# Linear attention with its gradients: eight stores issued by GpSimd instead of ScalarE, and a minimum moved from VectorE to GpSimd

## The chip, the cores and the metric

The kernel runs on one core of a Trainium2 chip. The metric is device time in microseconds (us) of one execution; a kernel's time is the median of its runs. In the profile PE is TensorE (PEld its weight loads), DVE is VectorE, ACT is ScalarE, POOL is GpSimd, and SP is SyncE, which computes nothing and issues transfers. ACTq, POOLq and SPq are the sequencers of these engines, which issue transfers.

## What is computed

The program takes two attention blocks over the same sequence length, S = 2048 rows of D = 448 columns, 16 heads of 28, and gives the output and all gradients in bfloat16.

```python
def _A_ref(x, wqkv, wo):                       # block A: linear attention
    qkv = split_heads(x @ wqkv)                # q, k, v
    phi = lambda t: jnp.where(t > 0, t + 1, jnp.exp(t)) + 1e-6
    pq, pk = phi(q), phi(k)
    kv = jnp.einsum("bhsd,bhse->bhde", pk, v)
    z = jnp.einsum("bhsd->bhd", pk)
    num = jnp.einsum("bhqd,bhde->bhqe", pq, kv)
    den = jnp.einsum("bhqd,bhd->bhq", pq, z)[..., None] + 1e-6
    return merge_heads(num / den) @ wo
def _B_ref(x, wq, wk, wv, wo):                 # block B: softmax attention, one k and v for all heads
    ...
out = concatenate([_A_ref(...), _B_ref(...)], axis=-1); grads = vjp(grad_out)
```

The listing is shortened from the reference (`split_heads` and `merge_heads` stand for its reshapes). Outputs: out_0 the forward result, out_1 the gradient of A's x, out_2 that of A_wqkv (448 x 1344: columns for q, k, v), out_3 that of A_wo, out_4 to out_8 those of block B. The change lies in block A: in the derivative of phi for q, and in the stores of the v columns of out_2 and of out_3.

## The kernel before

Block A is worked first (`phase_A`), then the projections of block B (`phase_B_pre`), then a long loop over block B's attention, forward and backward at once, in 512 steps, then B's remaining gradients. By the profile, A with the projections of B takes the first 210 us and the attention loop nearly all the rest. The sequence is cut into NS = 16 tiles of 128 rows. Each engine runs its own instructions strictly in order. Their order on each engine is set by a scheduler from the order of the program and the dependences, so instructions of neighbouring steps are interleaved; waits between engines go by semaphores. Work tiles come from small rotating pools: `psA` holds four PSUM buffers of each name ("agen" for products used at once, "aacc" for accumulators), `awk` three SBUF buffers of each name ("osb", "phiT"). A new tile waits until the readers of the tile that last had its buffer are done; where that reader is a store, until the store has landed.

The parts that the change and the prediction touch, in order of time:

- **Projections** (L270 to L287). For each tile `kproj` and, five tiles later, `qproj` multiply x by the weights (L236) into an "agen" buffer. `phi` takes the exponential on ACT (L241), its minimum with 1 plus 1e-6 on DVE (L243), and max(value, 0) plus that on DVE (L244), which also frees the PSUM buffer. For q the exponential stays in `wq_n` (the trace calls it wdq), and L262 replaces it there by its minimum with 1: that is the derivative of phi. `wq_n` is next read at L349 (`den_rx`), tile by tile.
- **kv and the denominators** (L282 to L364). `hilo` (L249 on ACT, L250 on DVE) takes the sums of phi(k) and x apart into two bfloat16 parts, `blkprod` multiplies them with the weights and masks the result on DVE (L301).
- **The loop over tiles** L399 to L411: forward result, the gradient of q, accumulated products.
- **Query gradient of the weights** (`gw(gqn, 0)`, L452), the gradient of k (L455 to L461, with L460 on DVE), loads for block B: B_x transposed by four transfers of SP (L467, issued at L115; the tile is called pk), B_wo by 16 loads (L474), four transposes of the gradient of k (L480, issued at L98; tile gaT).
- **Value and output weight gradients** (L481 to L497), four tiles i: `by_heads` (L484, matmuls at L313) gives the v columns of out_2; ACT evicts them into "osb" (L486) and issues the store (L487); matmuls with G (L493) give out_3; ACT evicts into "phiT" (L496) and issues the store (L497).
- **GpSimd's preparations for block B** (L499 to L515): memsets of `rep` (L501) and `wq_pad` (L502), 16 small copies (L505, L506), four copies (L509), memsets of `bsel` (L512, L515).
- **Key gradient of the weights** (`gw(gkn, 1)`, L524), evicted by ACT (L446, "osb" again, and L442) and stored by GpSimd (L447); then GpSimd loads B's output gradient into xa (L525, issued at L94). SP transposes rep and wq_pad (L522, L527).
- **Gradient of x** (L529 to L539): 11 matmuls a tile, evicted by ACT (L536), stored by GpSimd (L538).

Of the kernel before, what the change touches and what calls it, by code (L numbers as in the profile page):

```python
# [9 lines left out]
ALU = mybir.AluOpType  # L10
# [6 lines left out]
D = 448  # L17
P = 128
# [7 lines left out]
def kernel(  # L26
# [21 lines left out]
    nc = tc.nc  # L48
# [31 lines left out]
    def mm(out_ap, lhsT, rhs, start=True, stop=True):  # L80
        nc.tensor.matmul(out_ap, lhsT=lhsT, rhs=rhs, start=start, stop=stop, tile_position=(0, 0))  # L81
# [15 lines left out]
    def dma_T(dst, src, t0, n):  # L97
        nc.sync.dma_start_transpose(dst[:, t0:t0 + n, :, :].rearrange("p t c k -> p (t c) k"),  # L98
                                    src[:, t0:t0 + n, :].rearrange("p t d -> p (t d)"))
# [17 lines left out]
    def chunks_of(i):  # L117
        lo, hi = HR[i]
        return [k for k in range(4) if k * P < hi and k * P + DC_ROWS[k] > lo]
# [4 lines left out]
    def phase_A(pa, cA, cB, awk, psA):  # L124
        def gen(shape, dt=F32):
            return psA.tile(shape, dt, name="agen")
# [4 lines left out]
        def big(nm):  # L131
            return cA.tile([P, NS, 512], BF16, name=nm)

        xa, ga, pq, pk, wq_n, ppB = (big(n) for n in ("xa", "ga", "pq", "pk", "wdq", "pqpT"))
# [98 lines left out]
        def proj(st, off):  # L233
            ps = gen([P, D])
            for c in range(4):
                mm(ps[:, :], xaT[:, st, c, :], w3[:, c, off:off + D], start=(c == 0), stop=(c == 3))  # L236
            return ps

        def phi(ps, dst, E):

            nc.scalar.activation(out=E, in_=ps[:, :], func=ACT.Exp)  # L241
            tm = awk.tile([P, D], BF16, name="phiT")
            nc.vector.tensor_scalar(out=tm[:], in0=E, scalar1=1.0, scalar2=1e-6, op0=ALU.min, op1=ALU.add)  # L243
            nc.vector.scalar_tensor_tensor(out=dst, in0=ps[:, :], scalar=0.0, in1=tm[:], op0=ALU.max, op1=ALU.add)  # L244
# [14 lines left out]

        def qproj(st):  # L260
            phi(proj(st, 0), pq[:, st, 0:D], wq_n[:, st, 0:D])
            nc.vector.tensor_scalar(out=wq_n[:, st, 0:D], in0=wq_n[:, st, 0:D], scalar1=1.0, scalar2=None, op0=ALU.min)  # L262
            if st % 4 == 3:
                dma_T(tT, pq, st - 3, 4)

# [4 lines left out]
        for st in range(NS):  # L270
            if st + 2 < NS:
                xT(st + 2)
            kproj(st)
            if st >= 4:
                nc.scalar.activation(out=zero[st - 4], in_=zrow[:, :], func=ACT.Copy)
            if st >= 2:
                accmm(k1acc, xa, pk, st - 2)
            if st >= LAG:
                qproj(st - LAG)
# [6 lines left out]
        for st in range(NS - LAG, NS):  # L286
            qproj(st)  # L287
# [15 lines left out]
        def cols(t, k, i):  # L303
            if id(t) in blk_at:
                return blks[:, (blk_at[id(t)] + k) * D + i * P:(blk_at[id(t)] + k) * D + (i + 1) * P]
            return t[:, k, i * P:(i + 1) * P]

        def by_heads(ps, pairs):
            n = 4 * len(pairs)
            for m in range(n):  # L310
                lhs, rhs = pairs[m // 4]
                lo, hi = HR[m % 4]
                nc.tensor.matmul(ps[:, lo:hi], lhsT=lhs(m % 4), rhs=rhs[:, m % 4, lo:hi], start=(m == 0), stop=(m == n - 1),  # L313
                                 tile_position=(0, 0), skip_group_check=True)
# [166 lines left out]
        for i in range(4):  # L481
            r = DC_ROWS[i]
            ps = gen([P, D])
            by_heads(ps, [(lambda k: K1[0][:, i, k, :], dkv_blk), (lambda k: K1[1][:, i, k, :], dkv_blk)])  # L484
            sb = awk.tile([P, 512], BF16, name="osb")[:, 0:D]
            nc.scalar.activation(out=sb[0:r, :], in_=ps[0:r, :], func=ACT.Copy)  # L486
            nc.scalar.dma_start(out_2[i * P:i * P + r, 2 * D:3 * D], sb[0:r, :])  # L487
            ps = gen([P, 512])
            ks = chunks_of(i)
            n = 0  # L490
            for j in range(2):
                for k in ks:
                    mm(ps[:, :], cols(kv_blk, k, i), G[j][:, :, k, :], start=(n == 0), stop=(n == 2 * len(ks) - 1))  # L493
                    n += 1
            sb = awk.tile([P, D], BF16, name="phiT")
            nc.scalar.activation(out=sb[0:r, :], in_=ps[0:r, 0:D], func=ACT.Copy)  # L496
            nc.scalar.dma_start(out_3[i * P:i * P + r, :], sb[0:r, :])  # L497

        wq_pad = K1[0].rearrange("p c h k -> p c (h k)")  # L499
        rep = K1[1].rearrange("p c h k -> p (c h k)")[:, 0:1024].rearrange("p (w c k) -> p w c k", w=2, k=P)  # L500
# [6 lines left out]
        for c in range(4):  # L507
            r = slice(64 if c == 3 else 0, P)
# [131 lines left out]
    with ExitStack() as pa:  # L640
        cA = pa.enter_context(tc.tile_pool(name="cA", bufs=1, side="right"))
        cB = pa.enter_context(tc.tile_pool(name="cB", bufs=1, side="right"))
        awk = pa.enter_context(tc.tile_pool(name="awk", bufs=3, side="right"))
        io = phase_A(pa, cA, cB, awk, psA)
        pn3, shifts = phase_B_pre(pa, cA, awk, psA, io)
# [5 lines left out]
    with ExitStack() as cs_:  # L651
# [265 lines left out]
        with tc.manual_schedule():  # L917
            nc.sync.dma_start(wo, wo_d[:, 0:D].rearrange("(g p) c -> p g c", p=P))
            qX[0] = pqa_.tile([P, 4, 2, 512], BF16, name="qX")
            for g in range(4):  # L920
                st = pd_.tile([P, 2, 512], BF16, name="dsT").rearrange("p a (n j) -> p a n j", j=32).rearrange(
                    "p a (n b) j -> p (a n) b j", b=4)
# [3 lines left out]
            for u in range(NU + 28):  # L926
# [48 lines left out]
                if (b := due(u, 27)) is not None:  # L975
                    qc, pair, g, hp = blk(b)
                    nc.vector.tensor_scalar(out=qT_B[g][64 * hp:64 * hp + 64, qc * 256:(qc + 1) * 256],  # L977
                                            in0=oq[64:128, 0:256], scalar1=scale, scalar2=None, op0=ALU.mult)
# [20 lines left out]
                if u % 2:  # L999
                    b, i = divmod(u - 27, 8)  # L1000
# [25 lines left out]
                if u == 536:  # L1026
                    dk_sum = pd_.tile([P, 2, 512], BF16, name="dsT").rearrange("p a b -> p (a b)").bitcast(F32)
                    for c in range(2):
                        r = 64 * (1 - c)
# [5 lines left out]
                if 0 <= y < NU:  # L1035
                    b, tp = divmod(y, 8)
                    if tp == 0:
                        dsx[b] = px_.tile([P, 8, 2, 2, 256], BF16, name="dsx")
                    nc.vector.transpose(  # L1039
                        out=dsx[b][:, tp, :, :, :].rearrange("p h t c -> p (h t c)").bitcast(F32),  # L1040
# [15 lines left out]
        for c in range(4):  # L1056
# [4 lines left out]
                                           op0=ALU.mult, op1=ALU.add)  # L1061
# [47 lines left out]
        for c in range(4):  # L1109
            r = DC_ROWS[c]  # L1110
# [41 lines left out]
```

## Time and profile before

| | |
|---|---|
| runs (3) | 1057.06 us median, 1056.17 to 1061.49 |
| profiled execution | 1055.19 us, of which its span on the core 1053.5 |
| granted TensorE clock | 0.999 |
| busy in the span, PE, DVE, ACT, POOL | 1008.2, 898.1, 871.2, 772.8 us |
| 16 x L262 on DVE | 264 to 377 ns each, median 266; from 17.4 to 49.6 us |
| 40 to 60 us: PE, DVE busy of 20 us | 18.27, 18.98 |
| 120 to 140 us: PE, ACT, POOL busy of 20 us | 17.14, 5.06, 9.07 |
| DMA busy share, 100 to 180 us in steps of 20 | 1.03, 0.91, 1.09, 1.06 |

All lines of the profile are of one execution; times run from the start of its span. An instruction group shows engine, line and operation, out<-in and the shape. In brackets stands the idle time of the engine just before it, and what released it. The chain of work that ended last is followed back from the last instruction, at each step to what released it. The spans of GpSimd are rougher than those of the other engines.

### The profile page before, as it was taken

The page shows a single profiled execution, that of the slowest core. Times are in us where ns is not written, and L with a number is a line of the kernel's source. Part 1 is how long each engine was busy: PE and PEld are TensorE (multiplying, and loading weights), DVE is VectorE, ACT ScalarE, POOL GpSimd, SP SyncE. Part 2 cuts the span into 40 slices and gives each one's busy share as a digit, 9 for nine tenths or more (in the row PEclk, how much of TensorE's full clock was granted, in tenths as well). Part 3 has the DMA queues.
Part 4 walks back from the last instruction along what each step waited for, and adds up shares of the span by engine and source line. Part 5 has one row for each costly group of instructions (what it writes and reads, how often), then busy time and mean ns, then how long its engine had stood idle before and what let it go on. Part 6 is the DMA issues. An engine that isn't in the chain of part 4 may idle for free.

```text
span 1053.5 us, 40033 instructions
## 1 busy us (share of the span) xinstructions
PE 1008.2 (96%) x16245; PEld 485.7 (46%) x16245; DVE 898.1 (85%) x1797; ACT 871.2 (83%) x1743; POOL 772.8 (73%) x1020
## 2 busy tenths in 40 slices
PE   9999989998999999999999999999999999999997
PEld 5555545434444444444444444444444444444444
DVE  7897500669999999999999999999999999999942
ACT  6463122599999999999999999999999999999632
POOL 6001252238988998899899889988998999888860
PEclk9999999999999999999999999999999999999999
DMA  9879999089999999999999999999999999999972
GB/s 264 157 128 196 188 202 233 21 166 197 200 186 197 177 193 199 199 196 192 193 180 194 196 201 187 199 201 184 188 194 186 196 191 198 201 194 180 216 157 84
DMA packets 689730, 195.15 MB, mean 185 GB/s; under 512 B 670408, under 2 KB 687584, under 8 KB 689544
## 3 DMA queue, kind: packets, MB, share of 16 engines
q1 hardware_dynamic: 680392, 179.97, 101.7%
q0 software_dynamic: 4192, 8.66, 3.0%
q10 hardware_dynamic: 4960, 3.96, 1.2%
q8 instruction: 127, 2.08, 0.8%
q14 instruction: 59, 0.48, 0.2%
HBM read 12.60 MB, written 10.84 MB: 22 GB/s over the span
## 4 chain that ended last, share of the span: by engine, by line
PE 43%; ACT 33%; issue 14%; DVE 5%; POOL 3%; DMA 1%; ACTq 0%; DVEq 0%; SPq 0%; POOLq 0%
ACT cp L960 17%; ACT eT L992 13%; PE agen L81 13%; PE aacc L676 10%; PE agen L676 10%; PE aacc L81 6%; POOL dsT L961 2%; ACT eT L946 2%; PE aacc L809 2%; PE aacc L840 1%; DVE dsT L958 1%; DVE dsx L1039 1%; DMA pk<-in_B_x_dram 0%; DMA out_dram<-dsT 0%; PE aacc L85 0%
## 5 line engine op out<-in xcount | busy, mean ns | idle before, releaser
L961 POOL TENSOR_TENSOR dsT<-cp,eT 128x512 bf16<-128x512 bf16 x512 | 587.8, 1156 | 77.4 <-ACT cp L960 71.2
L1039 DVE STREAM_TRANSPOSE dsx<-dsT 128x512 f32<-128x512 f32 x512 | 357.6, 699 | 2.4 <-POOL dsT L961 0.2
L676 PEld LDWEIGHTS <-R 32*128 32x128 bf16 (+1 forms) x9104 | 228.3, 94 | 274.0 <-issue 238.9
L958 DVE TENSOR_TENSOR dsT<-agen,eT 128x512 bf16<-128x512 f32 x512 | 341.7, 667 | 10.3 <-PE agen L676 5.1
L960 ACT ACTIVATE cp<-agen 128x512 bf16<-128x512 f32 x512 | 314.9, 615 | 11.4 <-PE agen L676 10.3
L946 ACT ACTIVATE eT<-aacc 128x512 bf16<-128x512 f32 x512 | 313.2, 612 | 13.1 <-PE agen L676 4.1
L992 ACT ACTIVATE eT<-aacc 128x512 bf16<-128x512 f32 x512 | 321.0, 627 | 0.0
L676 PE MATMUL agen<-dsx,qX 32*32 32x512 bf16 x4024 | 264.1, 376 | 0.0
L676 PE MATMUL agen<-doT,R 32*128 32x256 bf16 x2048 | 246.5, 269 | 3.9 <-DVE dsT L958 2.4
L676 PE MATMUL aacc<-R,R 32*128 32x256 bf16 (+1 forms) x2240 | 218.2, 268 | 6.8 <-DVE oTs L819 1.9
L676 PE MATMUL agen<-eT,R 128*32 128x256 bf16 x2048 | 157.5, 274 | 0.1
L676 PE MATMUL agen<-dsT,R 128*32 128x256 bf16 x2048 | 156.6, 274 | 0.1
L676 PEld LDWEIGHTS <-qX 32*32 32x32 bf16 x4096 | 78.3, 89 | 111.7 <-issue 53.5
L676 PE MATMUL aacc<-eN,don 128*32 128x512 bf16 x1024 | 97.0, 379 | 0.0
L81 PEld LDWEIGHTS <-R 128*128 128x128 bf16 x517 | 40.9, 98 | 41.9 <-issue 11.8
L427 POOL COPY pk<-R 128x256 bf16<-128x256 bf16 x4 | 1.6, 398 | 71.4 <-DVE R L389 61.9
L81 PE MATMUL agen<-R,R 128*128 128x448 bf16 (+1 forms) x180 | 42.1, 361 | 0.5 <-DVE pq L244 0.3
L851 POOL COPY qst<-R 128x512 bf16<-128x512 bf16 x56 | 34.3, 613 | 3.6 <-DMA qX<-qst 3.5
L823 POOL TENSOR_TENSOR prod<-R,oTs 128x128 f32<-128x128 bf16 x64 | 27.5, 430 | 9.3 <-DVE oTs L819 9.3
L676 PEld LDWEIGHTS <-don 128*32 128x32 bf16 x1024 | 33.8, 97 | 0.7 <-issue 0.3
L586 DVE TENSOR_TENSOR osb<-R 32x512 bf16<-32x512 bf16 x4 | 1.7, 414 | 35.4 <-ACT R L583 35.4
L977 DVE TENSOR_SCALAR R<-agen 64x256 bf16<-64x256 f32 x64 | 27.3, 426 | 2.8 <-PE agen L676 0.8
(232 smaller groups left out, 954.4 us busy)
## 6 DMA issues: line engine op xcount, KB each, us to landing
out_dram<-osb ACTq DMA_DIRECT2D x19, 112.0 KB
eN<-eT SPq DMA_TRANSPOSE x128
xa<-in_A_x_dram SPq DMA_DIRECT2D x8, 224.0 KB
ga<-in_grad_out_dram SPq DMA_DIRECT2D x4, 448.0 KB
xa<-in_grad_out_dram POOLq DMA_DIRECT2D x4, 448.0 KB, 8.5
out_dram<-wdq POOLq DMA_DIRECT2D x8, 224.0 KB, 5.9
eT<-in_grad_out_dram SPq DMA_DIRECT2D x4, 448.0 KB
eT<-in_B_x_dram SPq DMA_DIRECT2D x4, 448.0 KB
```

The source lines that it names most:

```text
L81: nc.tensor.matmul(out_ap, lhsT=lhsT, rhs=rhs, start=start, stop=stop, tile_position=(0, 0))
L676: nc.tensor.matmul(out, lhsT=lhsT, rhs=rhs, start=start, stop=stop, tile_position=pos, skip_group_check=True)
L809: nc.tensor.transpose(onp[:, qb, :, :].rearrange("p h c -> p (h c)"), oTs[0:64, qb * P:(qb + 1) * P], identF[0:64, 0:64], tile_position=(0 ...
L823: nc.gpsimd.tensor_tensor(out=prod[b][:], in0=dnv, in1=os_, op=ALU.mult)
L851: eng.tensor_copy(out=st.rearrange("p (b s) a j -> p b s a j", s=2)[:, :, s, :, :], in_=src.unsqueeze(2).to_broadcast([P, 4, 4, 32]))
L946: nc.scalar.activation(out=eT(u)[:, 0, :], in_=sp[0][:, :], func=ACT.Exp, scale=scale)
L958: nc.vector.tensor_tensor(out=dst[:, 0, :], in0=dp[0][:, :], in1=ew[:, 0, :], op=ALU.mult)
L960: nc.scalar.activation(out=cp[:, :], in_=dp[1][:, :], func=ACT.Copy)
L961: nc.gpsimd.tensor_tensor(out=dst[:, 1, :], in0=cp[:, :], in1=ew[:, 1, :], op=ALU.mult)
L977: nc.vector.tensor_scalar(out=qT_B[g][64 * hp:64 * hp + 64, qc * 256:(qc + 1) * 256], in0=oq[64:128, 0:256], scalar1=scale, scalar2=None, ...
L992: nc.scalar.activation(out=eT(u)[:, 1, :], in_=sp[1][:, :], func=ACT.Exp, scale=scale)
L1039: nc.vector.transpose(out=dsx[b][:, tp, :, :, :].rearrange("p h t c -> p (h t c)").bitcast(F32), in_=dsT[y][:, :, :].rearrange("p h c -> p ...
```

## The change

In `qproj`, L262 runs on GpSimd instead of VectorE: it takes the minimum of the exponentials with 1 in place, for all 16 tiles. In the loop over the value and output weight gradients, the stores L487 and L497 are issued by GpSimd instead of ScalarE, eight in all. What is computed stays the same.

```diff
         def qproj(st):
             phi(proj(st, 0), pq[:, st, 0:D], wq_n[:, st, 0:D])
-            nc.vector.tensor_scalar(out=wq_n[:, st, 0:D], in0=wq_n[:, st, 0:D], scalar1=1.0, scalar2=None, op0=ALU.min)
+            nc.gpsimd.tensor_scalar(out=wq_n[:, st, 0:D], in0=wq_n[:, st, 0:D], scalar1=1.0, scalar2=None, op0=ALU.min)
...
             nc.scalar.activation(out=sb[0:r, :], in_=ps[0:r, :], func=ACT.Copy)
-            nc.scalar.dma_start(out_2[i * P:i * P + r, 2 * D:3 * D], sb[0:r, :])
+            nc.gpsimd.dma_start(out_2[i * P:i * P + r, 2 * D:3 * D], sb[0:r, :])
...
             nc.scalar.activation(out=sb[0:r, :], in_=ps[0:r, 0:D], func=ACT.Copy)
-            nc.scalar.dma_start(out_3[i * P:i * P + r, :], sb[0:r, :])
+            nc.gpsimd.dma_start(out_3[i * P:i * P + r, :], sb[0:r, :])
```

On each engine the order of the remaining instructions is the same as before, but for one pair on PE (weights and matmul of the masked product kvT, 128x168) that comes after the last q projection instead of before it. On GpSimd the 16 minima stand after the memset L564, ahead of the copies L427. The eight stores stand thus: the first two ahead of L501, three among the copies L505 and L506, and three between L502 and the last L506.

## The prediction

> **What bounds the kernel now.** I read the page first, then the waits by stage, then the timelines where a wait of PE stood.
>
> ```profile
> PE 1008.2 (96%) x16245; PEld 485.7 (46%) x16245; DVE 898.1 (85%) x1797; ACT 871.2 (83%) x1743; POOL 772.8 (73%) x1020
> PE 43%; ACT 33%; issue 14%; DVE 5%; POOL 3%; DMA 1%; ACTq 0%; DVEq 0%; SPq 0%; POOLq 0%
> ```
>
> The first line is busy time of each engine, the second the chain of work that ended last. PE is nearly always busy; DVE and DMA hold 5% and 1% of the chain. The change touches only the linear-attention stage, the first 210 us of 1053.5. There PE runs almost without a hole up to 210 us, and whatever follows takes its start from PE (the exponentials of the attention loop start at 210.35 us, after a matmul). So the change is worth the PE holes that it closes, less those that it opens. The two holes that matter stand in the waits of 128 to 138 us and in the chain of 40 to 52 us.
>
> ```profile
> ACT phiT L496 <- DMA pk<-in_B_x_dram: 4.5, 1, 4.5
> PE agen L81 <- ACT phiT L496: 2.9, 1, 2.9
> ```
>
> ```profile
> 129.43 0.54 ACT L486 ACTIVATE osb<-agen 128x448 bf16<-128x448 f32 x1 [2.55 <-PE agen L313]
> 134.04 0.34 ACTq L487 DMA_DIRECT2D out_dram<-osb  x1
> 134.48 0.55 ACT L496 ACTIVATE phiT<-agen 128x448 bf16<-128x448 f32 x1 [4.50 <-DMA pk<-in_B_x_dram]
> ```
>
> The first fence is the waits (total, times, longest); the second ACT's timeline. ACT evicts the first value-gradient tile at 129.43, and its next instruction is the issue of that tile's store. The issue goes out only at 134.04. In the program's instruction list it waits on a completion semaphore which the fourth transpose of B_x (L115, issued by SP at 129.34) also raises. Behind it stands the eviction L496, which frees one of the four "agen" PSUM buffers, and PE needs that buffer: PE stops after the third by_heads (131.59 + 0.63 = 132.2) and goes on at 135.07. That is 2.86 us by the timeline.
>
> ```profile
> 46.13 0.62 DVE pq L244
> 46.75 0.18 DVE wdq L262
> 46.93 0.37 DVE phiT L243 x2
> 47.30 0.53 DVE pq L244
> 47.84 0.18 DVE wdq L262
> 48.02 0.53 DVE pq L244
> 48.55 0.18 DVE wdq L262
> 48.73 0.18 DVE phiT L243
> 48.92 0.21 DVE blks L301
> 49.13 0.53 DVE pq L244
> 49.66 0.18 DVE wdq L262
> 49.84 0.25 DVE blks L301
> 50.14 1.53 PE aacc L81 x24
> ```
>
> This is the chain itself (start, length). From 43.6 to 50.1 us it lies on DVE: the last five q projections are finished there, and the first products of kv wait for L301 behind them. L262, the minimum that moves, is on the chain with 0.18 us a time (its duration is 0.27, but the next instruction starts 0.18 after it). PE's holes there are 0.32, 1.09 and 0.31 us.
>
> **The minimum, part by part.** Removed from DVE: 16 instructions of 0.27 us. Eleven lie in the loop of 17 to 42 us, where PE sets the pace (2.27 to 2.5 us an iteration) and DVE idles up to 0.53 us before L243: they gain nothing. Of the other five, the chain has 0.06 + 4 x 0.18 = 0.78 us.
>
> Added to GpSimd: 16 minima of 128x448 bf16. The trace has no such instruction there. The nearest rows are L509, a GpSimd copy of the same shape with one input, 0.562 us, and L190, a select, 0.553; the far end is L961, 128x512 with two inputs, 1.156. I take 0.56, the row of the same shape and number of inputs. GpSimd ends its setup at 18.6 us and does nothing until 72.2, so no instruction is queued behind the minima but the copies L427 (four, from 72.2). Their reader, L349, starts at 54.5 us; the last minimum, whose L243 is at 48.65, ends some 0.7 us after it. So the new wait of L349 is met before it comes up.
>
> The hidden price is that DVE's L243 may have to wait for GpSimd. The trace shows that such instructions do:
>
> ```profile
> 115.55 0.47 DVE L460 TENSOR_SCALAR phiT<-pk 128x448 bf16<-128x448 bf16 x1
> 116.46 0.26 DVE L460 TENSOR_SCALAR phiT<-pk 128x448 bf16<-128x448 bf16 x1
> 117.18 0.53 DVE L460 TENSOR_SCALAR phiT<-pk 128x448 bf16<-128x448 bf16 x1
> ```
>
> ```profile
> 115.42 0.47 POOL L454 MEMSET ga<- 64x448 bf16 x1
> 117.12 0.47 POOL L454 MEMSET ga<- 64x448 bf16 x1 [1.24 <-issue]
> ```
>
> L460 has L243's shape and kind. Alone it takes 0.26; begun under a GpSimd memset it ends 0.12 to 0.13 us after the memset does. L244 and L461, which read PSUM, show no stretch (0.60 to 0.62). So I lay the minima between the L243s. In the loop, a minimum starts when L243 of q ends and runs beside L244 (0.54 to the next start): it ends as the next L243 begins, costing nothing. In the tail, two L243 stand together, then two L244 (1.08 us), against two minima (1.12 us) that start after the second L243: L243 of tile 13 and of 15 may each slip by 0 to 0.1 us. With m for one minimum, the first L301 can't start before about 45.4 + 4m + 0.6 us: 48.2 for m = 0.56, against 48.1 from DVE alone and 48.84 now. I take a gain of **0.7 us**; the ends are 0.8 and, for m = 1.156, 50.6 - 48.8 = a loss of 1.8.
>
> [...]
>
> **The stores, part by part.** Removed from ACT: eight issues, 0.34 to 1.14 us each, and their waits. With L487 and L497 gone, L496 of tile 0 follows its matmul at about 130.0 and the PSUM buffer is free at 130.6, before PE asks at 132.2. What is late next? L486 and L496 of tiles 1 to 3 take 0.54 us each, against 1.2 us of PE work; nothing. The second stall of ACT (5.38 us before L496 at 145.06) hides under PE's 9.24 us of the key gradient and costs nothing already. The gain is the whole hole, **2.86 us**.
>
> Added to GpSimd: eight issues, by the L447 rows 0.55 us each, 4.4 us. In the instruction list the first two stand ahead of the memset L501, the next three among the copies L505/L506, the last three after the memset L502. Laid end to end from 130.0: L501 at 131.2, the last copies at 138.2, L502 to 140.0, the store of tile 3's value gradient at 141.1, L509 to 144.1, L515 to 146.8, the key gradient's stores to 149.0, the loads of xa (L94) 149.0 to 152.1. Now those loads issue at 150.65 to 153.7. Nothing is pushed back; rep (read by PE at 181.8) and wq_pad (read by SP's transposes at 161.4) keep 15 us or more. SP's queue keeps its order.
>
> New waits: the evictions L446 of the key gradient reuse "osb" buffers, and now wait for stores that GpSimd issued late. The third needs tile 3's store, issued at 141.1; stores of 112 KB from GpSimd landed in 3.7 us (median of L447's six), 4.8 in the stretch of 141 to 153 us, so at 146 against the 145.0 at which PE has the sum. One us is covered: behind these evictions stand L442 and the L536s, and PE has four PSUM buffers of 2.08 us each before it needs them. The cover ends at about 154 us, a landing 11 us after issue; the largest median landing of the trace's GpSimd groups is 8.5 (448 KB). So its cost runs from nothing to nothing within the rows.
>
> Do 3.6 us survive to the end? Transposes keep DMA full to 183 us and won't come sooner, but their readers have room: gkT's second transpose landed at 144.4, needed at 155; the transposes of B's output gradient are issued by 184, read at 211. The load of wo (209.8) follows PE. In the attention loop every transfer follows the loop's own engines, so its start carries through.
>
> **Sum.** 0.7 + 2.86 = 3.6 us. The profiled execution took 1055.19 us (span 1053.5 and 1.7 around it): 1051.6. It lay 1.9 under the median of the runs, 1057.06; against the median the forecast is 1057.06 - 3.6 = **1053.5**.
>
> **Rivals.** [...] (b) *The shift is lost*: a transfer that PE doesn't wait for now ends as late as before and PE waits for it before the loop: 1057. For it: DMA full from 100 to 183 us; against: the 10 to 25 us of room. A store that doesn't start sooner is no rival, since PE waits only for ACT. [...]
>
> **Chances.** Forecast 0.69, (a) 0.13, (b) 0.09, (c) 0.09. More than 4.6 us can't come from PE's holes (1.7 at 46 to 50, 2.9 at 132). A run of this kernel can tell about 0.5% (5.3 us) from no change; 3.6 is under that, but the runs scatter (1056.17 to 1061.49), and I give 0.23 to a measured gain past it, all of it out of the forecast's 0.69. So faster 0.23, within 0.5% 0.68, slower 0.09. Range: down to 1050.5 (4.6 us and 2 of scatter), up to 1057.3 for (a) and (b).
>
> **What would show it.** L496 of tile 0 near 129 us on ACT with no DMA before it, and no PE hole of 2.9; L85's second group about 3.6 us before 146.86; the first exponentials at 206.8 instead of 210.35. For the minimum: L262 on POOL at 0.56, L243's maximum after 20 us still under 0.4, PE's 1.09 us hole at 48 to 49 down to 0.3. Wrong if L262 takes over 1 us, if L446's third eviction waits past 150 us, or if the start of the loop moves and the end doesn't.

## The result, and the profile after

The changed kernel takes 1052.9 us (median of 11 runs, 1051.06 to 1055.12); the kernel before, run beside it, 1059.98 (11 runs, 1056.17 to 1062.75). The ratio is 0.9933, 95% interval 0.9919 to 0.9948: 7 us faster. The forecast was 1053.5. The profiled execution took 1052.68 us.

The page's busy times hardly differ, but for POOL (772.8 us before), which got the stores and the minima; the shares of the chain have moved by a point:

```profile
PE 1008.4 (96%) x16236; PEld 486.6 (46%) x16245; DVE 895.9 (85%) x1781; ACT 871.5 (83%) x1743; POOL 798.2 (76%) x1044
PE 44%; ACT 33%; issue 14%; DVE 6%; POOL 2%; DMA 0%; ACTq 0%; DVEq 0%; POOLq 0%
```

ACT's timeline (start, length, what; in brackets the idle time before and what ended it) has no issue left between the evictions:

```profile
129.78 0.54 ACT L486 ACTIVATE osb<-agen 128x448 bf16<-128x448 f32 x1 [2.55 <-PE agen L313]
130.38 0.54 ACT L496 ACTIVATE phiT<-agen 128x448 bf16<-128x448 f32 x1
...
146.03 0.54 ACT L446 ACTIVATE osb<-aacc 128x448 bf16<-128x448 f32 x1 [1.08 <-DMA out_dram<-osb]
```

L496 of tile 0 runs at 130.38 instead of 134.48. The last line is the new wait that the prediction named: the third eviction of the key gradient waits 1.08 us for a store that GpSimd issued late. PE doesn't feel it. PE's timeline, after:

```profile
131.94 0.63 PE L313 MATMUL agen<-R,K 128*128 128x140 bf16 x8
132.40 1.46 PE L81 MATMUL agen<-ga,blks 128*128 128x512 bf16 x6
...
135.02 9.24 PE L81 MATMUL aacc<-wdq,xa 128*128 128x448 bf16 x48
```

The same place before:

```profile
135.07 1.46 PE L81 MATMUL agen<-ga,blks 128*128 128x512 bf16 x6 [2.86 <-ACT phiT L496]
...
137.69 9.24 PE L81 MATMUL aacc<-wdq,xa 128*128 128x448 bf16 x48
```

The group at 132.40 follows the one at 131.94 without a gap; the key gradient's second half (L85) comes at 144.20 instead of 146.86. The hole is gone, PE waits for nothing from 128 to 150 us, and the key gradient starts at 135.02, before at 137.69. On POOL's timeline the moved stores lie within 0.6 us of where the prediction laid them:

```profile
130.62 0.56 POOL L487 DMA_DIRECT2D out_dram<-osb  x1 [4.03 <-ACT osb L486]
...
138.46 1.81 POOL L502 MEMSET K<- 128x2048 bf16 x1
...
140.74 0.55 POOL L487 DMA_DIRECT2D out_dram<-osb  x1
...
149.18 3.02 POOL L94 DMA_DIRECT2D xa<-in_grad_out_dram  x4
```

The minimum is another matter. First its group on POOL (durations in ns, lowest, median, highest), then POOL's and DVE's timelines where the last q projections are finished:

```profile
L262 POOL TENSOR_SCALAR wdq<-wdq x16: 1318/1323/1369, 18.6 to 51.3; 128x448 bf16<-128x448 bf16 x16
```

```profile
46.10 6.53 POOL L262 TENSOR_SCALAR wdq<-wdq 128x448 bf16<-128x448 bf16 x5 [2.52 <-DVE phiT L243]
```

```profile
47.31 0.81 DVE L243 TENSOR_SCALAR phiT<-wdq 128x448 bf16<-128x448 bf16 x2
...
49.11 0.30 DVE L243 TENSOR_SCALAR phiT<-wdq 128x448 bf16<-128x448 bf16 x1
49.34 0.29 DVE L301 TENSOR_TENSOR blks<-aacc,blkm 128x140 bf16<-128x140 f32 x1
```

One minimum takes 1.32 us on GpSimd, five times what it took on DVE, and five of them run back to back from 46.10 to 52.63. Yet DVE runs its L243s in those microseconds, one of them stretched to 0.63, and reaches the first L301 at 49.34, 3.3 us before the minima end. PE's holes there, 1.09 + 0.31 us, have become one of 0.68 (the first line is from before, the second from after):

```profile
49.18 0.65 PE L81 MATMUL aacc<-R,pqpT 128*128 128x140 bf16 x8 [1.09 <-DVE blks L301]
```

```profile
49.68 2.30 PE L81 MATMUL aacc<-R,pqpT 128*128 128x140 bf16 x32 [0.68 <-DVE blks L301]
```

The two profiles of before and after give -3.6 us from a common start: PE's instruction at 40.21 stands at 41.12 in this one (the start of the execution came 0.9 us later), and the first exponential at 207.68 instead of 210.35; 2.67 + 0.91 = 3.6, as forecast. Of this, 8.26 - 5.24 = 3.0 us lie between L486 of tile 0 and the key gradient, and 0.6 us, the minimum's share, lie before. The medians give 7. The experiments look for the other 3.4.

### The profile page after: what moved, and what is told of

The parts are those of the page before. It is cut to its first block, busy times and chain, and to the rows that moved or that the text cites. A ratio compares the mean times of both kernels' runs of the same rounds, so it can differ in the third digit from the quotient of the medians.

```text
span 1050.9 us, 40033 instructions
## 1 busy us (share of the span) xinstructions
PE 1008.4 (96%) x16236; PEld 486.6 (46%) x16245; DVE 895.9 (85%) x1781; ACT 871.5 (83%) x1743; POOL 798.2 (76%) x1044
## 3 DMA queue, kind: packets, MB, share of 16 engines
q0 software_dynamic: 4544, 9.46, 3.4%
q10 hardware_dynamic: 3936, 3.16, 1.0%
## 4 chain that ended last, share of the span: by engine, by line
PE 44%; ACT 33%; issue 14%; DVE 6%; POOL 2%; DMA 0%; ACTq 0%; DVEq 0%; POOLq 0%
ACT cp L960 17%; ACT eT L992 13%; PE agen L81 13%; PE aacc L676 10%; PE agen L676 10%; PE aacc L81 6%; ACT eT L946 2%; DVE dsT L958 2%; PE aacc L809 2%; DVE dsx L1039 2%; PE aacc L840 1%; POOL dsT L961 1%; DMA out_dram<-dsT 0%; PE agen L313 0%; PE agen L227 0%
## 5 line engine op out<-in xcount | busy, mean ns | idle before, releaser
L946 ACT ACTIVATE eT<-aacc 128x512 bf16<-128x512 f32 x512 | 313.6, 612 | 13.6 <-PE aacc L676 4.3
L262 POOL TENSOR_SCALAR wdq<-wdq 128x448 bf16<-128x448 bf16 x16 | 21.1, 1327 | 12.9 <-DVE phiT L243 12.9
L427 POOL COPY pk<-R 128x256 bf16<-128x256 bf16 x4 | 1.6, 399 | 37.7 <-DVE R L389 37.7
```

What stands on the lines that cost most here:

```text
L262: nc.gpsimd.tensor_scalar(out=wq_n[:, st, 0:D], in0=wq_n[:, st, 0:D], scalar1=1.0, scalar2=None, op0=ALU.min)
L946: nc.scalar.activation(out=eT(u)[:, 0, :], in_=sp[0][:, :], func=ACT.Exp, scale=scale)
```

## The experiments

**Theory (hole).** L487 of tile 0 waits for another engine's transfer, whose landing differs between executions, so the hole is longer in most executions than the 2.86 us of the one profiled. **Rivals:** the minimum is worth the rest; or GpSimd's way to memory is (by the pages, the eight stores' 0.80 MB went from queue q10, 3.96 MB before and 3.16 after, to q0, 8.66 and 9.46). The wait itself can be read in the program's instruction lists. There issues of SP and ACT draw on eight completion semaphores (DMAHW0 to DMAHW7) in turn, and the eight stores on ACT each wait for an earlier user of theirs. In the lines below, each transfer raises the DMAHW semaphore named there when it lands; the first one is the fourth transpose of B_x, and the store L487 of tile 0 waits for it (L496 behind it stood 4.50 us until that landing, by ACT's timeline before):

```
before: SP   L115 DmaTransposeAnt pk<-in_B_x_dram 128x2048 [waits DMAHW3_49,DVE_49]
        SP   L474 DMACopy R_63<-in_B_wo_dram 28x448 [waits DMAHW4_49]
before: ACT  L487 DMACopy out_dram<-osb 128x448 [waits DMAHW3_49,Activation_49]
```

**1. The kernel before again.** The experiments ran on four chips; each ratio is to the kernel before on the same chip.

> The kernel before, unchanged, run once more as if it were another: ratio 1.000, within 0.2%. It gives a second profiled execution of the same program. The theory of the hole (PE waits behind ACT's first store, and the hole's length follows the landing of the fourth B_x transpose, so it differs from execution to execution): ACT's wait at L487 and PE's hole before 135 us differ from 4.5 and 2.86 us, and the span moves with them. The rival (the hole is the same in every execution, and the rest of the measured gain is elsewhere): hole of 2.86 us again.

Measured: 1060.69 us, ratio 0.9999 (0.9986 to 1.0011). Its profile has a hole of 3.51 us, and something that the profile of before didn't have. Windows of 1 us of PE (length, busy, granted clock, DMA share, GB/s):

```profile
136.00:137.00 1.00, 0.16 (x1) 0.63 0.55 161
137.00:138.00 1.00, 1.00 (x3) 0.50 0.56 115
138.00:139.00 1.00, 1.00 (x4) 0.50 1.02 229
139.00:140.00 1.00, 1.00 (x11) 0.67 1.24 224
140.00:141.00 1.00, 1.00 (x8) 1.00 1.01 119
```

PE stands idle from 133.33; 2.9 us later the granted clock drops to a half, and stays there for 0.74 + 2 + 0.66 = 3.4 us, most of them behind the hole. Six matmuls that took 1.46 us in the first profile of before take 2.72 here:

```profile
136.84 2.72 PE L81 MATMUL agen<-ga,blks 128*128 128x512 bf16 x6 [3.51 <-ACT phiT L496]
...
140.84 9.24 PE L81 MATMUL aacc<-wdq,xa 128*128 128x448 bf16 x48
```

From L486 of tile 0 (130.55) to the key gradient (140.84) this execution takes 10.29 us; the first profile 137.69 - 129.43 = 8.26; the changed kernel 135.02 - 129.78 = 5.24. So the stage is worth 5.05 us here and 3.0 in the profile that the forecast was worked from.

**2. Stores alone.**

```diff
-            nc.scalar.dma_start(out_2[i * P:i * P + r, 2 * D:3 * D], sb[0:r, :])
+            nc.gpsimd.dma_start(out_2[i * P:i * P + r, 2 * D:3 * D], sb[0:r, :])
...
-            nc.scalar.dma_start(out_3[i * P:i * P + r, :], sb[0:r, :])
+            nc.gpsimd.dma_start(out_3[i * P:i * P + r, :], sb[0:r, :])
```

> Only the stores are moved to GpSimd; the minimum stays on DVE. Theory of the hole: nearly the whole measured gain, ratio 0.994 to 0.995 (6 us of 1060), with PE's hole at 132 us gone from the profile. Rival (the minimum is worth more in ordinary runs than the 0.6 us seen in the profile): about 3 us, ratio 0.997.

Measured: 1053.13 us, ratio 0.9932 (0.9915 to 0.9948). PE has no hole at 132 us, the clock is 1.00 in the stage, which takes 134.97 - 129.73 = 5.24 us: within the intervals the whole gain.

```profile
132.35 1.46 PE L81 MATMUL agen<-ga,blks 128*128 128x512 bf16 x6
...
134.97 9.24 PE L81 MATMUL aacc<-wdq,xa 128*128 128x448 bf16 x48
```

**3. Minimum alone.**

```diff
-            nc.vector.tensor_scalar(out=wq_n[:, st, 0:D], in0=wq_n[:, st, 0:D], scalar1=1.0, scalar2=None, op0=ALU.min)
+            nc.gpsimd.tensor_scalar(out=wq_n[:, st, 0:D], in0=wq_n[:, st, 0:D], scalar1=1.0, scalar2=None, op0=ALU.min)
```

> Only the minimum is moved to GpSimd; the stores stay on ACT. Theory of the hole: 0.6 us or less (ratio 0.9993 to 1.000), since the fourth transpose doesn't come sooner and PE's later hole grows by what is gained before it; PE's hole about 3.4 us where the transpose lands as in the first profile. Rival (the minimum is worth the rest): ratio 0.9965. In the profile L262 takes 1.32 us on GpSimd, L243 of the 13th tile up to 0.63.

Measured: 1059.49 us, ratio 0.9995 (0.9981 to 1.0009): no difference that can be told. PE's hole before kv shrinks as in the changed kernel (0.7 us in all); the other hole is 3.19 us, with the clock at a half from 136.0 to 139.4 and 2.72 us for the six matmuls. The rival that the minimum is worth the rest falls.

```profile
136.09 2.72 PE L81 MATMUL agen<-ga,blks 128*128 128x512 bf16 x6 [3.19 <-ACT phiT L496]
```

**4. Stores on ACT, but behind the evictions.** All eight stay on ACT and are issued after the last eviction (L496 of tile 3), from tiles that are not reused, in dead space of R2.

```diff
-            sb = awk.tile([P, D], BF16, name="phiT")
...
+            sb = R2[:, 2 * i + 1, 0:D]
+            last = nc.scalar.activation(out=sb[0:r, :], in_=ps[0:r, 0:D], func=ACT.Copy)
+        with tc.issue_after(last.ins):
...
+                nc.scalar.dma_start(out_3[i * P:i * P + r, :], R2[0:r, 2 * i + 1, 0:D])
```

> The stores stay with ACT, but ACT issues all eight only after its last eviction of this step; the eight tiles are put in a dead part of R2 so that no eviction waits for a store. Theory of the hole (it is the eviction queued behind the waiting issue that costs, whichever engine issues): the same gain as with the stores on GpSimd, ratio 0.994 to 0.995, no hole at 132 us; ACT then waits at its stores until about 147 to 150 us, under PE's four free PSUM buffers. Rival (what pays is that GpSimd's transfers take another way to memory, or that ACT issues nothing): less than half of that gain, ratio 0.998 to 1.000.

Measured: 1056.78 us, ratio 0.997 (0.9954 to 0.9985). The ratio lies between the two forecasts, and the gain is a little under half of the full one, so the time alone decides nothing. The trace does: the hole at 132 us is gone and the stage takes 5.29 us, with the stores still on ACT. So that hole came from the queue, not from GpSimd's way to memory. But the waits are only moved. The eight issues end at 153.57, not by 150, and what stood behind them is late:

```profile
154.15 1.42 ACT L446 ACTIVATE osb<-aacc 128x448 bf16<-128x448 f32 x3 [17.45 <-DMA R<-R]
```

L446 starts at 154.15 instead of 143.97, the evictions of the gradient of x (here L539) behind it, and PE gets a hole of 1.47 us that ends at 156.75:

```profile
156.75 0.92 PE L81 MATMUL agen<-KO,pq 128*128 128x448 bf16 x4 [1.47 <-ACT wdq L539]
```

The profile is of a run with a mean clock of 1.00 (1055.84 us). In 3 of the 10 runs it is 0.998 or less, and these are the three longest (1059.03 to 1061.34 us); no profile shows where they lose it.

**5. The hole, partly filled.** Eight matmuls that nothing reads go on PE into the hole of the kernel before; ACT's wait stays. The limit of some 3 us and the 3.5 us of half clock in the theory below are estimates from the profiles so far: the clock stayed at 1.00 after the hole of 2.86 us, and was at a half for 3.4 us after those of 3.19 and 3.51.

```diff
+            fill = psA.tile([P, D], F32, name="aacc") if i == 2 else None; [mm(fill[:, :], woT[:, 0, 0:P], dkv_blk[:, 0, :]) for _ in range(8 if i == 2 else 0)]; sb = awk.tile([P, 512], BF16, name="osb")[:, 0:D]
```

> The kernel before with eight matmuls of 448 columns (about 0.19 us each, 1.5 us in all; their product is read by nothing) put on TensorE just ahead of the matmuls that wait in the hole at 132 us. ACT's wait and the time at which the hole ends are not touched. Theory of hole and clock (an idle time over some 3 us makes the clock fall to a half for about 3.5 us, which costs some 1.3 to 1.9 us on top of the hole): the idle time shows at some 2 us instead of 3.2 to 3.5, every window of 1 us keeps a clock of 1.00, the six matmuls after the hole take 1.5 us instead of 2.7, and the time falls by 1 to 2 us: ratio to the kernel before 0.998 to 0.999. Theory that only the waiting counts: the hole's end stays and so does the time, ratio 1.000 within 0.001; if the half clock follows from something else than the idle time, it is still there from the end of the hole on.

Measured: 1059.25 us (1054.81 to 1063.25), ratio 0.9977 (0.9962 to 0.9992). The profile shows what was expected:

```profile
132.23 1.68 PE L81 MATMUL aacc<-R,blks 128*128 128x448 bf16 x8
135.63 1.46 PE L81 MATMUL agen<-ga,blks 128*128 128x512 bf16 x6 [1.72 <-ACT phiT L496]
```

Useless work made the kernel 2.4 us faster by the ratio (1.4 by the medians, 1.7 by the stage, 8.63 instead of 10.29): with 1.72 us of idle time the clock stayed at 1.00, and the six matmuls take 1.46 again. But in 4 of its 12 runs the mean granted clock was still 0.998 or less, which experiment 9 takes up.

**6. One store back on ACT.**

```diff
-            nc.gpsimd.dma_start(out_2[i * P:i * P + r, 2 * D:3 * D], sb[0:r, :])
+            (nc.scalar if i == 0 else nc.gpsimd).dma_start(out_2[i * P:i * P + r, 2 * D:3 * D], sb[0:r, :])
```

> The changed kernel with one store of the eight, that of the value weights' first tile (L487, i = 0), put back on ACT. Theory that a waiting issue blocks the engine's queue behind it: all of the loss comes back with this one store: L496 of tile 0 waits some 5 us behind a transfer of the tile pk, PE has a hole of 2.9 to 3.5 us at 132 us, the clock falls to a half after it where the hole is over 3 us, and the ratio to the kernel before is 0.998 to 1.001. Theory that each of the eight issues costs its share (eight issues of 0.35 to 1.1 us on ACT's queue): one eighth comes back, ratio 0.993 to 0.995.

Measured: 1060.82 us, ratio 0.9998 (0.9988 to 1.0009). One store of eight brings all of the loss back:

```profile
135.38 0.54 ACT L496 ACTIVATE phiT<-agen 128x448 bf16<-128x448 f32 x1 [4.99 <-DMA pk<-in_B_x_dram]
```

PE stands behind it:

```profile
135.97 2.09 PE L81 MATMUL agen<-ga,blks 128*128 128x512 bf16 x6 [3.34 <-ACT phiT L496]
```

The issue before L496 goes out at 134.94. PE's hole is 3.34 us and ends at 135.97; the clock is at a half from 136.6 to 140.0. The issue itself takes 0.34 us: its price is what it waits for and who stands behind it.

**7. Only the first tile's two stores on GpSimd**, the other six on ACT (both lines as in 6, with `nc.gpsimd if i == 0 else nc.scalar`).

> The kernel before with only the two stores of the first tile issued by GpSimd, the other six by ACT. Theory of the blocked queue: ACT's first issue is now L487 of tile 1, about 1.2 us later, and it waits for the same landing (some 135 to 136 us); behind it L496 of tile 1 waits, for which PE's matmuls of tile 3 wait. PE gets one more group (1.1 to 1.3 us of work) done first, so the hole shrinks from 2.9 to 3.5 us to 1.6 to 2.4 us and the clock stays at 1.00: some two thirds of the gain, ratio 0.994 to 0.997. Theory that the first store alone waits, whatever its place (that it stands for a wait of the queue that is over once): as the full change, ratio 0.993. Theory of equal shares: a quarter of the gain, ratio 0.998.

Measured: 1058.06 us, ratio 0.9974 (0.9962 to 0.9985), between the cases. None of the three theories had the mechanism: the first store on ACT is now another one, its turn among the eight semaphores is the next (DMAHW4 in the instruction list), and it waits for a load of B_wo that lands later than the transpose:

```profile
137.62 0.34 ACTq L487 DMA_DIRECT2D out_dram<-osb  x1
138.06 0.54 ACT L496 ACTIVATE phiT<-agen 128x448 bf16<-128x448 f32 x1 [5.88 <-DMA R<-in_B_wo_dram]
```

PE has done one group more by then, but the wait is longer too: the hole is 3.59 us (until 138.66), and the clock is at a half from 139.8 to 143.2, mostly while the key gradient runs, which takes 1.69 us longer for it (10.93 instead of 9.24):

```profile
138.66 1.02 PE L81 MATMUL agen<-ga,blks 128*128 128x512 bf16 x4 [3.59 <-ACT phiT L496]
139.51 10.93 PE L81 MATMUL aacc<-wdq,xa 128*128 128x448 bf16 x48
```

In the instruction lists of these kernels, what a store on this queue waits for goes by its number in the order of issues: the transpose in the kernel before (4.50 us), the load of B_wo here (5.88).

**8. The minimum twice.** The changed kernel, with L262 run twice for each tile (the second changes nothing).

```diff
-            nc.gpsimd.tensor_scalar(out=wq_n[:, st, 0:D], in0=wq_n[:, st, 0:D], scalar1=1.0, scalar2=None, op0=ALU.min)
+            for _ in range(2): nc.gpsimd.tensor_scalar(out=wq_n[:, st, 0:D], in0=wq_n[:, st, 0:D], scalar1=1.0, scalar2=None, op0=ALU.min)
```

> The changed kernel with the minimum of q's exponentials taken twice on GpSimd for each tile (the second changes nothing), so that it takes 2.6 us a tile instead of 1.32. Theory of the prediction (VectorE can't start one of its own operations while GpSimd holds the minimum, so the first masked product comes at 45.4 + 4 m + 0.6 us): at m = 2.6 it comes at 56.5 us instead of 49.3, L243 waits up to 2.6 us, and the time is 6 to 7 us longer than the changed kernel's, ratio to the kernel before 0.998 to 1.000. Theory that the minimum on GpSimd runs beside VectorE (as the trace of the change hints: L243 of 0.63 us at most while minima of 1.32 us run back to back): the first masked product stays near 49 to 50 us, L243 stays under 0.7 us, the last minimum ends near 60 us with nothing waiting for it, and the time is that of the changed kernel, ratio 0.993 within 0.0015.

Measured: 1054.35 us, ratio 0.9936 (0.9924 to 0.9948). GpSimd runs the last 17 minima without a gap from 39.20 to 61.93 us, and up to kv DVE isn't held back by them:

```profile
49.47 0.29 DVE L301 TENSOR_TENSOR blks<-aacc,blkm 128x140 bf16<-128x140 f32 x1
...
56.50 0.76 DVE L349 TENSOR_TENSOR wdq<-wdq,phiT 128x448 bf16<-128x448 bf16 x1
```

The first L301 comes at 49.47, where the prediction's formula has 45.4 + 4 x 2.65 + 0.6 = 56.6. L243 takes 0.65 us at most. What there is of a stretch comes later, on operations with two SBUF inputs: some L348 and L349 take 0.74 to 0.76 instead of 0.38, and the first L376 comes at 58.25 instead of 57.36. This isn't free: PE gets holes of 0.18, 0.23 and 0.49 us at 59 to 63 us, and L486 of tile 0 starts at 131.38 instead of 129.78. The median is 1.4 us above the changed kernel's; the intervals of the two ratios don't tell them apart.

**9. Sixteen idle-filling matmuls, and the kernel before once more.** As 5, with `range(16 if i == 2 else 0)`.

> As the kernel with eight idle-filling matmuls, but with sixteen (3.2 to 3.4 us; their product is read by nothing), which reach to within 0.5 us of the end of the shortest hole seen (2.86 us). Question: with eight of them a third of the executions still showed a granted clock of 0.998 or less. Theory that the hole's length differs between executions and reaches 5 us and more: with sixteen the idle time that is left is under 2 us in nearly all executions, the clock is 0.999 or 1.000 in all, and what is left of the loss is the hole alone: the time lies 3 to 5 us above that of the changed kernel, some 1056 to 1058 us, ratio 0.996 to 0.998. Theory that the clock falls for another reason than the idle time (something in the same microseconds that the stores on ACT also set off): some executions still show 0.998 or less, in the same share as with eight.

Measured: 1057.86 us, ratio 0.9972 (0.9959 to 0.9985); the clock is 0.999 or 1.000 in 11 of 12 runs. So at this place the half clock went with the idle time. In the profile 0.15 us of idle time is left:

```profile
136.28 1.45 PE L81 MATMUL agen<-ga,blks 128*128 128x512 bf16 x6 [0.15 <-ACT phiT L496]
```

What remains is the delay. By the stage it is 8.58 - 5.24 = 3.3 us, by the medians 1057.86 - 1052.9 = 5.0, by the ratios 4.1.

> The kernel before unchanged, profiled once more, for the length of the hole behind L487 of the first tile. Theory that the landing of the transfers that it waits for differs between executions: a hole between 2.8 and 5.5 us, other than 2.86 and 3.51, with the clock at a half after it if it is over 3 us. Theory that the hole has two lengths only: 2.9 or 3.5 again.

Measured: 1060.43 us in one execution; a hole of 3.45 us, the clock at a half from 136.2 to 139.6, stage 10.30 us.

**10. The delay without the wait.** The changed kernel with 26 such matmuls in that place: all that follows comes as late as in the kernel before, but PE is busy and no issue of ACT waits. (The edit is that of 5, with 26, in the changed kernel.) Beside it the changed kernel again.

> The changed kernel with 26 matmuls of 448 columns (5.1 to 5.4 us; their product is read by nothing) put on TensorE ahead of the same six matmuls, so that all that follows comes as late as in the kernel before, but with TensorE busy, ACT's queue free and the clock at 1.00. Question: the kernel before loses some 5.0 us in this stage by its profiles (hole and half clock), but 7 us by the medians. Theory that the loss is what the stage shows and the rest lies with executions whose hole is longer: this kernel takes 5.1 to 5.4 us more than the changed one, some 1058 us, ratio to the kernel before 0.9975 to 0.9985. Theory that a later start of the attention loop alone lengthens the loop (its stalls fall differently): ratio 0.9995 to 1.001, and the loop takes 844 to 846 us from its first exponential to the end instead of 843.

> The changed kernel once more, on the same chip as the shifted one, as the zero for it: ratio to the kernel before 0.993 within 0.0015, no hole at 132 us, clock 1.00, a loop of 842.5 to 843.3 us. A longer loop here (844 and more) would show that the loop's length varies by itself.

Measured: 1058.11 us, ratio 0.9973 (0.9958 to 0.9987), and 1053.03 us, ratio 0.9931 (0.9912 to 0.995). The difference is 5.1 us; the 26 matmuls delay the key gradient by 10.16 - 5.24 = 4.9:

```profile
132.61 5.08 PE L81 MATMUL aacc<-R,blks 128*128 128x448 bf16 x26
...
140.15 9.24 PE L81 MATMUL aacc<-wdq,xa 128*128 128x448 bf16 x48
```

Within the intervals a delay here goes through to the end one for one, and a later start of the attention loop costs nothing by itself. The loop took 845.5 us here, as the second theory said, but it took 844.4 in the changed kernel too: its length varies by itself.

All profiles side by side, in us: the stage runs from the start of L486 of tile 0 to the key gradient's first matmul, the loop from the first exponential (L946) to the end of the span.

| kernel | PE's hole | clock after it | stage | loop | median |
|---|---|---|---|---|---|
| before, first profile | 2.86 | 1.00 | 8.26 | 843.2 | 1059.98 |
| before again (1) | 3.51 | 0.50 | 10.29 | 844.9 | 1060.69 |
| before again (9) | 3.45 | 0.50 | 10.30 | 845.4 | one run |
| minimum alone (3) | 3.19 | 0.50 | 10.20 | 842.7 | 1059.49 |
| one store back (6) | 3.34 | 0.50 | 10.41 | 846.6 | 1060.82 |
| first two moved (7) | 3.59 | 0.50 | 8.98 | 842.0 | 1058.06 |
| 8 fillers (5) | 1.72 | 1.00 | 8.63 | 842.2 | 1059.25 |
| 16 fillers (9) | 0.15 | 1.00 | 8.58 | 844.5 | 1057.86 |
| 26 fillers, changed (10) | none | 1.00 | 10.16 | 845.5 | 1058.11 |
| stores on ACT, late (4) | none | 1.00 | 5.29 | 843.6 | 1056.78 |
| stores alone (2) | none | 1.00 | 5.24 | 843.1 | 1053.13 |
| changed | none | 1.00 | 5.24 | 843.2 | 1052.9 |
| changed again (10) | none | 1.00 | 5.24 | 844.4 | 1053.03 |
| minimum twice (8) | none | 1.00 | 5.24 | 842.5 | 1054.35 |

In the row of experiment 7 the stage leaves out the 1.7 us that the half clock costs behind its end. The loop's length scatters from 842.0 to 846.6 us with no link to the change; the longest, of one store back, holds a second stretch of half clock, from 276.6 to 280.0 us. The mean clock was recorded for every run, and says how often the clock fell: of 102 runs of the kernel before, 20 have 0.999 or more (median 1058.5 us), 45 have 0.998 (1060.4) and 37 less (1062.0); of 28 runs of kernels without the hole (changed, again, stores alone, minimum twice), 27 have 0.999 or more.

**What stays open.** The stage shows 5.05 of the 7 us, and the minimum's 0.6 us makes 5.7. That lies inside the interval of the gain (5.5 to 8.6 us), so this comparison alone doesn't show that anything is missing. But all 102 runs of the kernel before have a median 7.7 us above that of the 17 runs of the changed kernel, and most kernels in which an issue of ACT waits lie, by the ratios, 0.8 to 1.7 us further from the changed one than their stage says (one store back: 5.2 us by the stage, 6.9 by the ratios). Experiment 7 doesn't: 5.4 us with the half clock behind its stage, 4.3 by the ratios. Nor does the kernel that only comes later.

A part of the rest is probably a second stretch of half clock. In the profiles, runs with one stretch have a mean clock of 0.998, and the one with two, of one store back, has 0.996. Of the 102 runs of the kernel before 14 have 0.996 or less, of the 11 with one store back 6: going by the profiles, these had more than one. But the 20 runs of the kernel before with 0.999 or more lie 5.5 us above the changed kernel, and a stage like that of the first profile, with the minimum, gives 3.6. So the clock isn't all of it. A wait that is longer in ordinary executions than in the few profiled ones would do it; no profile here shows one.

## Why the prediction was right in the time and wrong in the gain

- **What bounds the kernel, and that the hole is behind ACT's waiting issue:** right. Experiments 2, 4 and 6 show it, down to the one instruction.
- **The stores' term, 2.86 us:** the step that failed, by its size. It took the hole of one execution for the hole of the kernel, and counted only idle time. In four more profiles of this queue the hole is 3.19 to 3.51 us, and each is followed by half a clock: the stage is worth 5.0 to 5.2 us, not 3.0. The sentence "more than 4.6 us can't come from PE's holes" fails by the same: it left out that what follows a hole can be slower (here six matmuls of 2.72 us instead of 1.46).
- **What GpSimd does with the stores:** right, with every instruction within 0.6 us of its place; L94 starts at 149.18 (laid at 149.0). L446's third eviction waits 1.08 us (one was forecast) and it costs nothing, since PE has four buffers before it. That this cover ends at about 154 us is borne out by experiment 4, where L446 at 154.15 opened a hole of 1.47 us.
- **The minimum's duration, m = 0.56:** wrong, and past the prediction's own sign of being wrong (L262 over 1 us); 1.32, beyond the dearest row that I took for the far end (1.156). A copy of the same shape with one input was not a near row for a `tensor_scalar`.
- **The formula for the first L301, 45.4 + 4 m + 0.6:** wrong too. At m = 1.32 it puts the first L301 at 51.3 and predicts a loss; it came at 49.34, and at m = 2.65 at 49.47. What GpSimd's memsets did to L460 (0.47 and 0.53 us instead of 0.26, ending 0.12 to 0.13 us after the memset) its minima didn't do to L243: beside 1.32 us minima back to back no L243 took more than 0.65 us, so none was held back for a whole minimum. The chances of (a) and (c), 0.13 and 0.09, stood for a loss by slow minima, which the ratio of the minimum alone does not show. The gain of 0.7 came out as 0.6 by luck: two errors cancelled. L243 reached 0.63 us where under 0.4 was forecast, and PE's hole of 1.09 us shrank to 0.68, not to 0.3. In time it is too small to be told (0.9995, 0.9981 to 1.0009).
- **The sum:** 1053.5 against 1052.9, and this is luck: a gain too small by 3.5 us (3.6 against 7.1) was taken from a start too low by 2.9 (1057.06 against 1059.98). The three runs of before that were shown had a median of 1057.06; the 102 of the experiments have 1060.6. That the median lay 1.9 us above the profiled execution was seen, but only carried along as an offset; it was the first sign that this execution was a lucky one. The gain of over 0.5% that was measured had a chance of 0.23.

At this place of the kernel half a clock came with the holes of 3.19 to 3.59 us, and not with those of 2.86, 1.72 and 0.15. So the cost of a hole of 2.86 us could jump in an execution where it is longer; the prediction didn't weigh it.

## What to carry to other kernels

Here a transfer's issue stood in its engine's queue and waited like any instruction, also for another engine's transfer whose completion semaphore it happened to share (L496 behind it stood 4.50 to 5.88 us); put such an issue where nothing urgent stands behind it, and look at what each issue waits for, not at how many there are. Holes of PE of 3.19 to 3.59 us cost 5.0 to 5.4 us here, more than their length, so look at the granted clock in the microseconds after a hole, and take its length from several executions before it becomes a term of a sum. An operation that the trace doesn't show on an engine wants a far end well beyond the nearest row (here 1.32 us against 0.56).

## What the runs showed of the hardware

- The stretch of half clock at PE's hole lasted 3.4 us in each of the five profiles that show one (1, 3, 6, 7, 9). It began 2.9 to 3.1 us after PE went idle in three profiles (1, 3, 9) and 0.7 and 1.2 us after PE had gone on in two (6 and 7).
- A `tensor_scalar` minimum of 128x448 in bfloat16 took 1.32 us on GpSimd and 0.27 on DVE; a copy of that shape took 0.56 on GpSimd. Beside such minima DVE's L243 went on (0.63 us at most in the changed kernel, 0.65 with the minimum twice), and with the minimum twice some of DVE's two-input operations took twice as long (0.76 instead of 0.38).
- The clock fell after short holes too. In the attention loop of the changed kernel's second profile it followed a hole of 1.10 us (windows as above):

```profile
269.00:270.00 1.00, 0.05 (x4) 1.00 0.79 168
270.00:271.00 1.00, 1.00 (x16) 0.68 1.15 62
271.00:272.00 1.00, 1.00 (x12) 0.50 1.27 231
```

The window of 269 us holds the hole; the clock falls in the next one. A hole of 1.15 us in the loop did the same in experiment 6, one of 1.07 in experiment 10 did not, nor did one of 1.19 at 862 us in experiment 6. What tells them apart stays open, so the length of a hole alone does not say whether the clock falls.
